# Loads issued when their buffers come free, and paired vector work, in a block-sparse attention and MoE kernel

## The chip, the cores and the metric

The kernel runs on one core of a Trainium2 chip. A time is the device time of one execution in microseconds (us); the time of a kernel is the median over its runs. Within a trace, times are counted from the first profiled instruction ("at 66.9" means 66.9 us after it), and the span is the time from there to the last one. The core has a matrix engine (TensorE, PE in the profile, with its weight loads as PEld), a vector engine (VectorE, DVE), an activation engine (ScalarE, ACT), a general one (GpSimd, POOL) and a queue that only issues transfers (SyncE, SP). Transfers run on 16 DMA engines.

## The reference

Four batches of 8 heads, 768 tokens, head size 64. Each token attends to the tokens less than 16 away and to 24 block rows: the maximum of the keys, and the mean of the values, over each block of 32 tokens. The result goes through a two-layer MLP with the quick GELU.

```python
B, H, S, D = q.shape                       # 4, 8, 768, 64
block, window = (32, 16)
k_sum = k.reshape(B, H, nb, block, D).max(axis=3)
v_sum = v.reshape(B, H, nb, block, D).mean(axis=3)
scores_l = scale * np.matmul(q, k.transpose(0, 1, 3, 2))
mask_l = np.abs(pos[:, None] - pos[None, :]) < window
scores_s = scale * np.einsum('bhsd,bhnd->bhsn', q, k_sum) + np.log(block)
a = softmax(concatenate([where(mask_l, scores_l, -1e9), scores_s]))
attn = np.matmul(a, concatenate([v, v_sum]))
h = x @ w_in                               # x = attn as (3072, 512); w_in 512 x 2048
out = (h * (1.0 / (1.0 + np.exp(-1.702 * h)))) @ w_out
```

All inputs are float32 in memory; all but the first keys are cast to bfloat16 or float16 as they are loaded.

## The kernel before

**Layout.** Heads go in four pairs p. For one batch, `kxs[s]` holds the transposed keys of all pairs as 12 tiles of 128 columns: 64 own columns, 32 halo columns copied from the neighbour tiles, and 24 block maxima in the rest (`s` is the batch modulo 2, so there are two such buffers, and likewise `qTs[s]` for queries and `vw[s]` for values). In `vw[s]` the halo rows and the block sums lie on the partitions beside the tile's own 64 tokens. One score product for a tile of 64 queries is then 64 columns, and one value product reads one such tile.

**Per batch,** the steps are: load k, q and v from memory with a cast; transpose keys and queries; fill the key halos and maxima (`rest_k`); fill the value halos by DMA (`halo_dmas`, four transfers), sum the value blocks on PE (`vsum`) and DVE (`block_sums`), and copy the sums into `vw[s]` by DMA (`sum_dmas`, two transfers); scores, exponential (ACT), mask (DVE), values (PE), norm (DVE), transposition of the result; first MLP layer (`ff_in`, `ff_one`), GELU (ACT), second layer (`ff_out`, `product`). `value_rows(s)` (line 1065) is the three steps on the values.

**Order.** Every engine's instructions run in the order in which they stand in the program (`_Ordered`, line 18), and each instruction waits only for what it reads or overwrites. So the attention of batch b+1 is written in between the MLP of batch b: in slots beside the second layer (`plan`, `beside`) and after blocks of the first layer (`todo` for batch 1, the loop from line 1112 for batches 2 and 3). In that loop `n // 2` counts eight blocks of the first layer, and `i` the 21 products of the second.

**Loads.** All k, q and v loads go out on POOL's queue: four transfers for k and q each, twelve for v (`load_turned`, `load_v`). POOL's queue is in order too, and no more than eight of its transfers are under way: each waits for the one eight before it. The buffers of k and q (`kb2`, `qb2`) are two tiles each, one per group g of two pairs, so a load of the next batch into group g waits until that group is transposed. `load_batch(b)` (line 242) issues k, v and q of a batch in a row. For batch 3 it holds them with small POOL copies that read a tile written later ("gates"): k waits for the query transpositions of batch 2 (`qTs[0]`), and q, issued in the loop (line 1133), for a result transposition (`xTT[1][1]`).

**Transpositions.** Batches 0 and 1 transpose on PE (`tk`, `tq`). Batches 2 and 3 use transposing DMAs on SP: `xk(g, s)` is two for the keys of a group, `xq(g, s)` one for its queries. SP also issues the halos, the block sums, the transpositions of results (`dx`) and the stores of the output, in order.

**Operand sums.** The second layer of batches 1 to 3, and most of the first of batch 3, work on sums of operands that save one product in eight: `g_sums(j)` (line 679) makes four sums of 128 x 384 for column block j on DVE, and `win_sum`, `w_sum` those of the weights.

Of the kernel before, what the change touches and what calls it, by code (L numbers as in the profile page):

```python
# [9 lines left out]
F32 = mybir.dt.float32  # L10
BF16 = mybir.dt.bfloat16
F16 = mybir.dt.float16
AX = mybir.AxisListType
# [22 lines left out]
def kernel(  # L36
# [82 lines left out]
    def load_turned(x, b, t2, name, gs_=(0, 1)):  # L119

        for g in gs_:
            t2[g] = castp2.tile([128, 2, NJ, 2, D], BF16, name=name, tag=name)
            for hh in range(2):
                h0 = hh * NP + 2 * g
                pool.dma_start(out=t2[g][:, :, :, hh].rearrange("p i a d -> p (i a) d"),
                               in_=x[b, h0:h0 + 2].rearrange("h (a p) d -> p (h a) d", p=128))

    def load_v(b):
        w5 = vw[b % 2].rearrange("p (j e) h c -> p j e h c", e=2)
        src = v[b].rearrange("h (j e p) d -> e j p h d", e=2, p=64)  # L130
# [108 lines left out]
        for g in range(4):  # L239
            eng.memset(v6[g * 32:g * 32 + nb, :, g, D:D + 1], float(block))  # L240

    def load_batch(b):
        if b == 3:
            pool.tensor_copy(out=gate2, in_=qTs[0][:, 0, 0:1])
        load_turned(k, b, kb2, "kb")
        if b == 3:
            pool.tensor_copy(out=gate2, in_=qTs[0][:, NP - 1, 0:1])
        if b == 1:
            load_turned(q, b, qb2, "qb", (0,))
        load_v(b)  # L250
        if b < 3:
            load_turned(q, b, qb2, "qb", (1,) if b == 1 else (0, 1))

    def load_w_in(n0, n1):
        wi = moe_w_in.rearrange("(ko ki) n -> ki ko n", ki=128)
# [82 lines left out]
    def at(ap, start, dims):  # L338
        a = ap[:, start:start + 1]
        return bass.AP(tensor=a.tensor, offset=a.offset, ap=[a.ap[0]] + dims)  # L340

    def flat_kx(p, s):
        return kx[p][s].rearrange("p t c -> p (t c)")

    def key_rows(p, s, ks, eng=dve, j0=0):
# [205 lines left out]
    def tk(p, s, eng):  # L551
        ps = psb.tile([128, 2048], BF16, name="ps_t", tag="big")[:, 0:S]
        turn_tiles(ps, kb2[p // 2][:, p % 2], NJ)
        copy(eng, at(flat_kx(p, s), 0, [[256, NJ], [192, 2], [1, 64]]),
             ps.rearrange("p (j e c) -> p j e c", e=2, c=64))
        rest_k(p, s, pool)

    def tq(p, s, eng):
        ps = pmm.tile([128, 1024], BF16, name="ps_t", tag="mm")[:, 0:S]
# [14 lines left out]
    def rest_k(p, s, eng=dve):  # L574
        ks = attp.tile([128, nb], BF16, name="ks", tag="ks")
        dve.tensor_reduce(out=ks.rearrange("p (j e n) -> p j e n", e=2, n=2),
                          in_=at(flat_kx(p, s), 0, [[256, NJ], [192, 2], [block, 2], [1, block]]),
                          axis=AX.X, op=ALU.max)
        key_halos(p, s, eng)
        key_rows(p, s, ks, eng)  # L580

    a_sb, x_sb, x2 = {}, {}, {}

# [13 lines left out]
    def values(b, half, g):  # L597

        if b == 1:
            banks = [pmm.tile([128, 512], F32, name="ps_av", tag="mm") for i in range(2)]  # L600
        else:
            ps = psb.tile([128, 1024], F32, name="ps_av", tag="big")
            banks = [ps[:, i * 512:i * 512 + 512] for i in range(2)]
        pvs = []
        for i in range(2):
            p = 2 * g + i
            a = a_sb[half, p]
            pv = banks[i][:, 0:390].rearrange("p (h j c) -> p h j c", h=2, j=JH)
            pvs.append(pv)
            for hh in range(2):  # L610
                for j in range(JH):
                    for e in range(2):
                        t = 2 * j + e
                        pe.matmul(out=pv[e * 64:e * 64 + 64, hh, j, :], lhsT=a[:, hh, t, :],
                                  rhs=vw[b % 2][:, half * TH + t, p + hh * NP if b else 2 * p + hh, 0:D + 1],
                                  start=True, stop=True, skip_group_check=True)
        x2[g] = attp.tile([128, 2, JH, 2, D], F16, name="x2", tag="x2", bufs=4)
        for i in range(2):
            norm(x2[g][:, :, :, i].rearrange("p h j d -> p j h d") if b else x2[g][:, i], pvs[i])

# [55 lines left out]
        gelu(half, nt, ph)  # L676


    def g_sums(j, eng=dve, which=(0, 1, 2, 3)):

        a1, a2 = gTb[:, j], gTb[:, j + NT // 2]
        l, r = slice(0, HALF), slice(HALF, S)
        for w in which:
            a, b_, op = {0: (a1[:, r], a2[:, r], ALU.add), 1: (gs[:, 0, j], a1[:, l], ALU.subtract),
                         2: (a1[:, l], a1[:, r], ALU.subtract), 3: (a2[:, l], gs[:, 1, j], ALU.subtract)}[w]
            eng.tensor_tensor(out=gs[:, w, j], in0=a, in1=b_, op=op)

    N1 = d_model // 2

# [180 lines left out]
            sp.dma_start(out=out[r0:r0 + 128, :], in_=osb)  # L870

    gate = consts.tile([128, 2], F32, name="gate")
    gate2 = consts.tile([128, 1], BF16, name="gate2")
    gate3 = consts.tile([128, 2], F32, name="gate3")
    dve.memset(gate, 0.0)

# [137 lines left out]
        key_rows(p, 0, ks0[:, p, 0:nb], dve, JH)  # L1014
    dve.memset(vw[1][:, :, :, D:VC], 1.0)
    clear_values(dve, 1)
    load_batch(1)


    plan0 = {1: ["q0", "q1", "q2"], 2: ["q3", "s0", "s1"], 4: ["s2", "s3"], 6: ["v0", "v1"], 8: ["x0"], 9: ["x1"]}  # L1020
# [63 lines left out]
    for i, (ms, part) in enumerate((ms, part) for part in range(4) for ms in range(JH)):  # L1084
        ff_out(0, ms, part)
        beside0(i)
        if i in (10, 11):
# [1 line left out]
            w_sum(i - 10, 1)  # L1089

    todo = {3: [lambda: tk(0, 1, act)], 4: [lambda: w_sum(2, 0)], 5: [lambda: tk(1, 1, act)],
            6: [lambda: w_sum(2, 1)], 7: [lambda: w_sum(3, 0)], 8: [lambda: tk(2, 1, act)], 
            10: [lambda: w_sum(3, 1)], 9: [lambda: tq(0, 1, dve)], 11: [lambda: tk(3, 1, act)], 12: [lambda: tq(1, 1, dve)],
            15: [lambda: value_rows(1)]}
    ff_in(1, range(3))
    for nt in range(3, NT):
        ff_in(1, (nt,))
# [4 lines left out]
    for i, (ms, part) in enumerate((ms, part) for ms in range(JH) for part in range(4)):  # L1102
        ff_out(1, ms, part)
        beside(1, i)
        if i == 2:
            load_batch(2)
        if i in (9, 11):
            xk(i // 2 - 4, 0)


    halves[0] = True
    for b in range(1, B - 1):
        nxt = b + 1 < B
        s = (b + 1) % 2
        if b == B - 2:
            for w in range(4):
                win_sum(w)
        for n in range(0, NT, 2):
            if n == 0:
                ff_open(order2[0:4], (lambda: tx(1, 1)) if b == 1 else None)  # L1120
            elif n == 2:
                for nt in order2[0:4]:
                    ff_one(1, nt)
                g_sums(0)
                g_sums(1)
            else:
                for nt in order2[n:n + 2]:
                    for half in range(2):
                        ff_one(half, nt)
                g_sums(n // 2, dve, (0, 1) if n + 2 == NT else (0, 1, 2, 3))  # L1130
            if nxt:
                if n == 0 and b > 1:
                    pool.tensor_copy(out=gate2, in_=xTT[1][1][:, 1, 0:1])
                    load_turned(q, b + 1, qb2, "qb")
                if n // 2 == 1:
                    value_rows(s)
                if n // 2 == 2 * b:
# [106 lines left out]
```

## Time and profile before

| | |
|---|---|
| median of 3 runs | 206.86 us (206.62 to 208.16) |
| the profiled execution | 206.51 us |
| its span, first to last instruction | 204.8 us |
| granted TensorE clock, mean | 0.998 |
| busy: PE, PEld, DVE, ACT, POOL | 198.1, 137.4, 140.4, 124.6, 92.7 us |
| moved by DMA | 27.93 MB, 95,851 packets, 83,649 of them under 512 bytes |

A busy figure is a sum of stretches in which an engine executes; matmuls overlap, and their ends are modelled. "Idle before" is the time in which an engine stood still before an instruction, with what ended it. The view of waits groups that by pairs of waiting and awaited work. The chain goes back from the last instruction to whatever released each step. The view of stretches gives the busy time of each engine in a piece of the span. A timeline row gives start, length, engine, operation, what is written and read, and a count. For a DMA the row shows its issue; the time to landing is from there to the last byte.

Stages by the trace: attention of the first token half of batch 0 until about 20 us; first layer on that half to 30; its second layer, with the attention of the other half beside it, to 45; first layer on the other half to 58, with the transpositions of batch 1; its second layer to 75, with the attention of batch 1; first layer of batch 1 to 97, with the keys and values of batch 2 made ready; products of batch 1 to 119, with the attention of batch 2; the same for batch 2 to 141 and 164; batch 3 to the end.

### The profile page before, as it was taken

What the parts mean: (1) busy time and instruction counts of PE and PEld (TensorE: products, weight loads), DVE (VectorE), ACT (ScalarE), POOL (GpSimd) and SP (SyncE); (2) the same over time, 40 slices, a digit from 0 to 9 for tenths busy, and PEclk for the clock granted to TensorE, in tenths of its full rate; (3) what the DMA queues carried; (4) which work ended last, traced back from release to release, by engine and by line L of the source; (5) the groups of instructions that cost most, each with busy time, mean ns of one, the idle gap of its engine ahead of it and who ended that gap; (6) DMA issues with size and microseconds to landing.
All of it is one profiled execution on the core that took longest, in us unless ns stands there. A gap on an engine that the chain in (4) does not pass through costs nothing.

```text
span 204.8 us, 5857 instructions
## 1 busy us (share of the span) xinstructions
PE 198.1 (97%) x2364; PEld 137.4 (67%) x2364; DVE 140.4 (69%) x388; ACT 124.6 (61%) x238; POOL 92.7 (45%) x144
## 2 busy tenths in 40 slices
PE   6989999999999999999999999999999999999992
PEld 6667654556754566665888975657888865578881
DVE  6767894594856874897768689896759546658211
ACT  4385876638786717777871546778661467983220
POOL 7965389555999584002965035000000019990000
PEclk9999999999999999999999999999999999999999
DMA  5999999999999999999999989996023730000222
GB/s 117 153 159 202 207 211 213 195 156 232 134 143 151 177 176 168 159 175 132 123 196 127 154 151 142 122 261 137 0 106 90 160 111 3 0 0 3 102 102 104
DMA packets 95851, 27.93 MB, mean 136 GB/s; under 512 B 83649, under 2 KB 92881, under 8 KB 95825
## 3 DMA queue, kind: packets, MB, share of 16 engines
q0 software_dynamic: 69920, 13.44, 85.2%
q1 hardware_dynamic: 25904, 14.13, 33.2%
q8 instruction: 18, 0.29, 0.6%
q14 instruction: 9, 0.07, 0.1%
HBM read 27.26 MB, written 6.29 MB: 164 GB/s over the span
## 4 chain that ended last, share of the span: by engine, by line
PE 90%; DMA 4%; POOL 2%; DVE 1%; issue 1%; ACT 0%; POOLq 0%; DVEq 0%
PE ph L28 33%; PE poA L28 16%; PE po L28 11%; PE poB L28 7%; PE ps_av L28 4%; DMA v0n<-in_v_dram 4%; PE poC L28 4%; PE phA L28 4%; PE ps_s L28 3%; PE ps_t L28 1%; PE ps_x L28 1%; POOL kb L28 1%; PE phB L28 1%; PE phC L28 1%; PE phE L28 1%; PE ps_vs L28 1%
## 5 line engine op out<-in xcount | busy, mean ns | idle before, releaser
L28 PE MATMUL ph<-xT,w_in_sb 128*128 128x384 f16 x416 | 70.2, 326 | 0.1
L28 PEld LDWEIGHTS <-w_in_sb 128*128 128x128 f16 x452 | 43.7, 98 | 27.8 <-issue 0.2
L28 ACT ACTIVATE gT<-ph 128x384 f16<-128x384 f32 x104 | 49.9, 492 | 18.5 <-PE ph L28 18.1
L28 PEld LDWEIGHTS <-gT 128*128 128x128 f16 x312 | 28.8, 98 | 11.3 <-issue 0.2
L28 ACT ACTIVATE a_sb<-ps_s 128x768 bf16<-128x768 f32 (+1 forms) x32 | 25.0, 826 | 12.5 <-PE ps_s L28 12.5
L28 POOL DMA_DIRECT2D vw<-in_v_dram x36 | 24.6, 700 | 12.4 <-DMA kb<-in_k_dram 4.8
L28 PEld LDWEIGHTS <-gs 128*128 128x128 f16 x288 | 27.7, 98 | 3.4
L28 POOL TENSOR_TENSOR gs<-gT 128x384 f16<-128x384 f16 x9 | 8.2, 911 | 42.3 <-ACT gT L28 42.3
L28 PE MATMUL po<-w_out_sb,gT 128*128 128x512 f16 x96 | 23.6, 380 | 0.0
L28 DVE TENSOR_TENSOR a_sb<-a_sb,mk 128x768 bf16<-128x768 bf16 x28 | 14.9, 554 | 6.5 <-ACT a_sb L28 5.9
L28 PE MATMUL poA<-ws,gs 128*128 128x256 f16 x144 | 18.7, 273 | 0.0
L28 DVE TENSOR_TENSOR x<-ps_av,rc 128x384 f16<-128x384 f32 x32 | 17.8, 558 | 1.1
L28 DVE TENSOR_TENSOR gs<-gT 128x384 f16<-128x384 f16 (+1 forms) x34 | 13.4, 394 | 7.2 <-ACT gT L28 6.9
L28 POOL DMA_DIRECT2D qb<-in_q_dram x16 | 15.1, 956 | 1.8 <-DMA w_in_sb<-in_moe_w_in_dram 1.1
L28 POOL DMA_DIRECT2D kb<-in_k_dram x15 | 14.5, 976 | 0.9 <-POOLq L1228 0.8
L28 PEld LDWEIGHTS <-kx 64*128 64x128 bf16 (+1 forms) x372 | 9.4, 95 | 6.8 <-issue 4.4
L28 DVE TENSOR_REDUCE ks<-kx 128x24 bf16<-128x768 bf16 x12 | 11.4, 949 | 3.4 <-ACT kx L28 3.2
L28 ACT ACT_TABLE_LOAD x10 | 12.8, 1283 | 1.0 <-PEq L1228 0.8
L28 ACT ACTIVATE osb<-poA 128x256 f32<-128x256 f32 x9 | 3.5, 384 | 16.0 <-PE poA L28 16.0
L28 ACT ACTIVATE s<-poA 128x256 f32<-128x256 f32 x11 | 4.2, 386 | 11.2 <-PE poA L28 11.2
L28 PEld LDWEIGHTS <-a_sb 128*64 128x64 bf16 (+2 forms) x400 | 7.8, 108 | 2.8 <-issue 1.3
L28 PE MATMUL poA<-ws,gT 128*128 128x256 f16 x72 | 9.3, 273 | 0.0
(117 smaller groups left out, 282.7 us busy)
## 6 DMA issues: line engine op xcount, KB each, us to landing
out_dram<-osb SPq DMA_DIRECT2D x23, 256.0 KB, 3.3
kb<-in_k_dram POOLq DMA_DIRECT2D x15, 192.0 KB, 7.1
qb<-in_q_dram POOLq DMA_DIRECT2D x12, 192.0 KB, 10.9
vw<-in_v_dram POOLq DMA_DIRECT2D x36, 64.0 KB, 5.7
w_out_sb<-in_moe_w_out_dram POOLq DMA_DIRECT2D x4, 512.0 KB, 13.0
w_in_sb<-in_moe_w_in_dram POOLq DMA_DIRECT2D x3, 512.0 KB, 12.9
vw<-vs SPq DMA_DIRECT2D x6, 198.0 KB, 6.1
v0n<-in_v_dram POOLq DMA_DIRECT2D x4, 192.0 KB, 8.1
```

The lines of the kernel that those rows point to most:

```text
L28: r = f(*a, **kw)
```

## The change

- `load_batch` and both gates are gone. `load_k(b, g...)`, `load_q(b, g...)` and `load_v(b)` are called where the buffers come free. Batch 1's loads keep place and order. Batch 2: v before the first layer of token half 1 of batch 0, k after the transpositions of batch 1's keys (group 0 at block 7, group 1 at block 12 of that layer), q in the place where `load_batch(2)` was. Batch 3: k and q in the first layer of batch 1 (`n // 2` = 0 and 2), v where `load_batch(3)` was.
- On SP, `xk` for batches 2 and 3 stands after products 4 and 7 of the second layer (it was 9 and 11, and 16 and 18), and both `xq` at the start of the next first layer, ahead of `value_rows` (they were at `n // 2` = 2 and 4, behind it).
- `rest_k` (one pair) becomes `rest_k2` (two pairs at once): one maximum over 128 x 1536 and three halo copies on DVE, then one `key_rows` per pair on DVE. For batch 1, halos and rows were on POOL, and the four calls stood in `tk`; now two calls stand at blocks 7 and 13.
- `g_sums` can make two column blocks at once: blocks 0 and 1, 2 and 3, 4 and 5 are paired. `values` for batches 2 and 3 norms two pairs with one reciprocal and one product.

```diff
-    def load_batch(b):
-        if b == 3:
-            pool.tensor_copy(out=gate2, in_=qTs[0][:, 0, 0:1])
-        load_turned(k, b, kb2, "kb")
-        if b == 3:
-            pool.tensor_copy(out=gate2, in_=qTs[0][:, NP - 1, 0:1])
...
+    def load_k(b, *gs_):
+        load_turned(k, b, kb2, "kb", gs_)
+
+    def load_q(b, *gs_):
+        load_turned(q, b, qb2, "qb", gs_)
...
+    def rest_k2(g, s):
+        flat = kxs[s].rearrange("p i t c -> p (i t c)")
+        o, n = 2 * g * NQ * 128, 2 * NJ
+        ks = attp.tile([128, 2, nb], BF16, name="ks", tag="ks")
+        dve.tensor_reduce(out=ks.rearrange("p i (j e n) -> p (i j) e n", e=2, n=2),
+                          in_=at(flat, o, [[256, n], [192, 2], [block, 2], [1, block]]),
+                          axis=AX.X, op=ALU.max)
+        dve.tensor_copy(out=at(flat, o + 256 + 96, [[256 * NJ, 2], [256, NJ - 1], [1, 16]]),
+                        in_=at(flat, o + 256 - 16, [[256 * NJ, 2], [256, NJ - 1], [1, 16]]))
...
+        for i in range(2):
+            key_rows(2 * g + i, s, ks[:, i])
...
              ps.rearrange("p (j e c) -> p j e c", e=2, c=64))
-        rest_k(p, s, pool)
...
+        if b > 1:
+            pv = ps.rearrange("p (i c) -> p i c", i=2)[:, :, 0:390].rearrange("p i (n c) -> p i n c", c=D + 1)
+            rc = attp.tile([128, 2, 2 * JH, 1], F32, name="rc2", tag="rc2")
+            dve.reciprocal(out=rc, in_=pv[..., D:D + 1])
+            dve.tensor_mul(x2[g].rearrange("p h j i d -> p i (h j) d"), pv[..., 0:D],
+                           rc.to_broadcast([128, 2, 2 * JH, D]))
+            return
...
-    load_batch(1)
+    load_k(1, 0, 1)
+    load_q(1, 0)
+    load_v(1)
+    load_q(1, 1)
...
-            6: [lambda: w_sum(2, 1)], 7: [lambda: w_sum(3, 0)], 8: [lambda: tk(2, 1, act)], 
-            10: [lambda: w_sum(3, 1)], 9: [lambda: tq(0, 1, dve)], 11: [lambda: tk(3, 1, act)], 12: [lambda: tq(1, 1, dve)],
+            6: [lambda: w_sum(2, 1)], 8: [lambda: tk(2, 1, act)], 
+            7: [lambda: w_sum(3, 0), lambda: rest_k2(0, 1), lambda: load_k(2, 0)],
+            10: [lambda: w_sum(3, 1)], 9: [lambda: tq(0, 1, dve)], 11: [lambda: tk(3, 1, act)],
+            12: [lambda: tq(1, 1, dve), lambda: load_k(2, 1)], 13: [lambda: rest_k2(1, 1)],
             15: [lambda: value_rows(1)]}
+    load_v(2)
     ff_in(1, range(3))
...
         if i == 2:
-            load_batch(2)
-        if i in (9, 11):
-            xk(i // 2 - 4, 0)
+            load_q(2, 0, 1)
+        if i in (4, 7):
+            xk(i // 3 - 1, 0)
...
-                g_sums(0)
-                g_sums(1)
+                g_sums(0, n=2)
...
-                g_sums(n // 2, dve, (0, 1) if n + 2 == NT else (0, 1, 2, 3))
+                if n // 2 in (3, 5):
+                    g_sums(n // 2 - 1, n=2)
+                elif n // 2 > 5:
+                    g_sums(n // 2, dve, (0, 1) if n + 2 == NT else (0, 1, 2, 3))
             if nxt:
-                if n == 0 and b > 1:
-                    pool.tensor_copy(out=gate2, in_=xTT[1][1][:, 1, 0:1])
-                    load_turned(q, b + 1, qb2, "qb")
+                if n == 0:
+                    xq(0, s)
+                    xq(1, s)
+                    if b == 1:
+                        load_k(3, 0, 1)
                 if n // 2 == 1:
                     value_rows(s)
-                if n // 2 == 2 * b:
-                    xq(0, s)
-                    xq(1, s)
-                if n // 2 in (2, 3, 4, 5):
-                    rest_k(n // 2 - 2, s)
+                if n // 2 == 2 and b == 1:
+                    load_q(3, 0, 1)
+                if n // 2 in (2, 4):
+                    rest_k2(n // 4 - 1, s)
...
             if nxt and b + 2 < B:
                 if i == 1:
-                    load_batch(b + 2)
-                if i in (16, 18):
-                    xk(i // 2 - 8, b % 2)
+                    load_v(b + 2)
+                if i in (4, 7):
+                    xk(i // 3 - 1, b % 2)
```

More of the change, by code (lines that the diff above doesn't have):

```diff
@@ L240, in clear_sums @@
             eng.memset(v6[g * 32:g * 32 + nb, :, g, D:D + 1], float(block))
-    def load_batch(b):
-        if b == 3:
-            pool.tensor_copy(out=gate2, in_=qTs[0][:, 0, 0:1])
-        load_turned(k, b, kb2, "kb")
-        if b == 3:
-            pool.tensor_copy(out=gate2, in_=qTs[0][:, NP - 1, 0:1])
[L248 to L252, printed above, removed]
+    def load_k(b, *gs_):
+        load_turned(k, b, kb2, "kb", gs_)
+    def load_q(b, *gs_):
+        load_turned(q, b, qb2, "qb", gs_)
     def load_w_in(n0, n1):
@@ L343, in flat_kx @@
         return kx[p][s].rearrange("p t c -> p (t c)")
+    def rest_k2(g, s):
[7 more added lines that the diff above has]
+                        in_=at(flat, o + 256 - 16, [[256 * NJ, 2], [256, NJ - 1], [1, 16]]))
+        dve.tensor_copy(out=at(flat, o + 128 + 48, [[256 * NJ, 2], [256, NJ - 1], [1, 16]]),
+                        in_=at(flat, o + 256, [[256 * NJ, 2], [256, NJ - 1], [1, 16]]))
+        dve.tensor_copy(out=at(flat, o + 128 + 32, [[256, n], [-48, 2], [1, 16]]),
+                        in_=at(flat, o + 48, [[256, n], [144, 2], [1, 16]]))
+        for i in range(2):
+            key_rows(2 * g + i, s, ks[:, i])
     def key_rows(p, s, ks, eng=dve, j0=0):
@@ L572, in xq @@
                      in_=qb2[g].rearrange("p i a h d -> p (i a h d)"), transpose=True)
[L574 to L580, printed above, removed]
     a_sb, x_sb, x2 = {}, {}, {}
@@ L676, in ff_one, with g_sums @@
         gelu(half, nt, ph)
-    def g_sums(j, eng=dve, which=(0, 1, 2, 3)):
-        a1, a2 = gTb[:, j], gTb[:, j + NT // 2]
+    def g_sums(j, eng=dve, which=(0, 1, 2, 3), n=1):
+        j1, j2 = slice(j, j + n), slice(j + NT // 2, j + NT // 2 + n)
+        a1, a2 = gTb[:, j1], gTb[:, j2]
         l, r = slice(0, HALF), slice(HALF, S)
         for w in which:
-            a, b_, op = {0: (a1[:, r], a2[:, r], ALU.add), 1: (gs[:, 0, j], a1[:, l], ALU.subtract),
-                         2: (a1[:, l], a1[:, r], ALU.subtract), 3: (a2[:, l], gs[:, 1, j], ALU.subtract)}[w]
-            eng.tensor_tensor(out=gs[:, w, j], in0=a, in1=b_, op=op)
+            a, b_, op = {0: (a1[:, :, r], a2[:, :, r], ALU.add), 1: (gs[:, 0, j1], a1[:, :, l], ALU.subtract),
+                         2: (a1[:, :, l], a1[:, :, r], ALU.subtract),
+                         3: (a2[:, :, l], gs[:, 1, j1], ALU.subtract)}[w]
+            eng.tensor_tensor(out=gs[:, w, j1], in0=a, in1=b_, op=op)
     N1 = d_model // 2
@@ L872 @@
     gate = consts.tile([128, 2], F32, name="gate")
-    gate2 = consts.tile([128, 1], BF16, name="gate2")
     gate3 = consts.tile([128, 2], F32, name="gate3")
```

## The prediction

> **What bounds the kernel now.** The first view is the page's row of busy times.
>
> ```profile
> PE 198.1 (97%) x2364; PEld 137.4 (67%) x2364; DVE 140.4 (69%) x388; ACT 124.6 (61%) x238; POOL 92.7 (45%) x144
> ```
>
> PE is busy nearly throughout, but busy matmuls can still be waiting ones, so the next two views ask whether PE ever waits: its own waits, in full, and the stretches.
>
> ```profile
> PE ps_h L28 <- DVE warm L28: 1.3, 1, 1.3
> PE ps_vt L28 <- DMA v0n<-in_v_dram: 0.6, 1, 0.6
> PE ps_s L28 <- DVE qT L28: 0.4, 1, 0.4
> PE ps_k L28 <- ACT kb L28: 0.3, 1, 0.3
> ```
>
> ```profile
> 76.00:97.00 21.00, 21.00 (x184) 12.65 (x183) 15.86 (x54) 14.89 (x31) 4.17 (x6) 1.00 1.65 159
> ...
> sum 180.00, PE 179.56 PEld 123.47 DVE 126.05 ACT 113.61 POOL 77.22; mean PE 19.95 PEld 13.72 DVE 14.01 ACT 12.62 POOL 8.58
> ```
>
> PE waits four times in the whole run, each time for something of batch 0: the warm-up tile, the first keys, the first values, and its late queries. The sum covers 20 to 200 us: 0.44 us of 180 are idle. The clock of the stretch is 1.00. Last, the chain in order of time, for the pace and for the dates by which something must be ready.
>
> ```profile
> 34.18 0.57 DVE qT L28
> ...
> 80.74 0.53 PE ps_vs L28 x48
> 81.27 15.71 PE ph L28 x96
> 96.98 0.46 PE ps_s L28 x24
> ...
> 108.83 0.88 PE ps_av L28 x48
> ```
>
> The late queries' wait is at 34, ahead of the first changed instruction. 96 matmuls of 384 columns in 15.71 us are 164 ns each, that is 2.3 columns a nanosecond with nothing between them. This stretch is where DVE is fullest and where the DMAs of batch 2 run, and neither slows it. So **PE's own instructions are the time**; a wait that goes on another engine is worth nothing unless PE stood behind it.
>
> The Trainium skill, page "Perfetto Trace Analysis", section "Identifying the Most-Contended Engine", says that matmul busy time doesn't tell how near PE is to its limit and that weight-load busy time (here PEld) should be used. By it 67% would leave a third of PE's time open to better feeding. The trace disagrees at 164 ns a matmul; what the rule would make of the time is the third rival.
>
> **The change part by part.** It removes, adds or reorders no PE instruction from the first to the last: the transposes, scores, sums and products stand in the same slots. So the gain is bounded by the idle 0.44 us between 20 and 200, none of it behind a changed instruction: I take 0 (bounds 0 and -0.4). What is left to price is whether something arrives later than PE asks for it.
>
> *Operand sums, norms, later halos.* The groups of DVE between 84.5 and 96.9, and one group of the whole run.
>
> ```profile
> L28 DVE TENSOR_REDUCE ks<-kx 128x24 bf16<-128x768 bf16 x4 | 3.8, 948 | 0.0
> L28 DVE TENSOR_TENSOR gs<-gT 128x384 f16<-128x384 f16 x10 | 3.5, 354 | 0.6 <-ACT gT L28 0.5
> L28 DVE COPY kx<-kx 128x80 bf16<-128x80 bf16 x8 | 1.0, 172 | 0.0
> L28 DVE COPY kx<-ks 128x288 bf16<-128x288 bf16 x4 | 0.9, 230 | 0.0
> L28 DVE COPY kx<-kx 128x192 bf16<-128x192 bf16 x4 | 0.8, 196 | 0.0
> ```
>
> ```profile
> L28 DVE TENSOR_TENSOR a_sb<-a_sb,mk 128x768 bf16<-128x768 bf16 x28 | 14.9, 554 | 6.5 <-ACT a_sb L28 5.9
> ```
>
> A two-input operation of 768 columns takes 554 ns (the masks), two of 384 take 708. Merging four pairs saves 0.6 us, and with three merges in each of two batches 3.7 us of DVE. The norm merge is alike and smaller. All of it is hidden under PE: priced at 0. The pairing delays the sums of blocks 2 and 4 by one block, but the products that read them come after block 7, so nothing waits.
>
> *Batch 1's key maxima and halos leave POOL for DVE.* The rows of POOL, DVE, SP and PE in order of time show what they held up and what follows.
>
> ```profile
> 53.45 2.04 POOL L28 DMA_DIRECT2D qb<-in_q_dram  x2
> 55.53 0.75 POOL L28 COPY kx<-kx 128x80 bf16<-128x80 bf16 x3
> ...
> 59.76 4.05 POOL L28 DMA_DIRECT2D kb<-in_k_dram  x4
> ```
>
> ```profile
> 56.51 0.55 DVE L28 COPY qT<-ps_t 128x768 bf16<-128x768 bf16 x1
> 58.23 0.29 DVE L28 COPY vpart<-ps_vs 128x128 f32<-128x128 f32 x1 [1.18 <-PE ps_vs L28]
> 58.56 1.18 DVE L28 TENSOR_TENSOR vs<-ps_vs,vpart 32x128 bf16<-32x128 f32 x4
> ```
>
> ```profile
> 55.53 2.69 SPq L28 DMA_DIRECT2D vw<-vw  x4
> 59.77 1.24 SPq L28 DMA_DIRECT2D vw<-vs  x2
> ```
>
> ```profile
> 55.20 0.50 PE L28 MATMUL ps_t<-wide,qb 128*128 128x128 bf16 x6
> ...
> 60.30 0.50 PE L28 MATMUL ps_t<-wide,qb 128*128 128x128 bf16 x6
> ...
> 66.93 0.57 PE L28 MATMUL ps_av<-vw,a_sb 128*64 128x65 bf16 x24
> ```
>
> DVE's second query copy is held by PE's transposes, which end at 55.7, so it runs 55.75 to 56.3 (today at 56.51, behind a single maximum). The second paired maximum follows it. No row has that shape; its cost lies between one of today's, 0.95, and two, 1.90, and I take 1.8, near two, because the copies above show time growing with columns. The three copies cost 0.5 to 1.1 (once or twice 2 x 0.172 + 0.196), I take 0.6; two key rows 0.46. That is 2.9 us: DVE is free at 59.2, and the block sums (0.29 + 1.18) end at 60.7 instead of 59.74. The first of the two copies of sums into the value buffer leaves at 60.7, the second at 61.35 (half of 1.24 later).
>
> *Twelve value loads of batch 2 move ahead of its keys.* POOL is free at 55.5 instead of 59.76 and starts them there, twelve at 0.7 us each (24.6 for 36 in the row below), to 63.9, then the keys' four (4.05, to 68) and the queries' four (to 72). No instruction of PE needs them before 80.7. What they meet are the transfers that PE does need: batch 1's four value halos (issued 55.5 to 58.2) and the two sums, which must have landed when the values start at 66.93. The rows for the loads and, one query each, for three pairs of sums:
>
> ```profile
> L28 POOL DMA_DIRECT2D vw<-in_v_dram x36 | 24.6, 700 | 12.4 <-DMA kb<-in_k_dram 4.8
> ```
>
> ```profile
> DMA to landing us min/median/max: 3.0/4.3/5.6
> DMA to landing us min/median/max: 5.3/5.5/5.7
> DMA to landing us min/median/max: 9.0/9.3/9.7
> ```
>
> The first query is these two sums today: the first met almost no load (3.0), the second the first key load (5.6), and it landed at 66.0, 0.9 us ahead of PE. The second is batch 0's sums, half as large, under a full stream of loads; the third is batch 2's, behind four halos and two transposing DMAs. After the change the second sum leaves at 61.35, and with 5.6 to 6.2 it lands between 66.95 and 67.55. PE then waits 0 to 0.6 us; **I take 0.3**. The ends are 0 (at 5.5 it is just in time) and 4.1 (at 9.7, 71.05); I stay near 5.5 because no transposing DMA is ahead of these two.
>
> A rule bears on that end. The Trainium skill's page "DMA: Bandwidth & Descriptors", section "Queues, rings and completion order", says that each DMA engine takes turns between the queues at packet granularity. By it loads on POOL's queue could at most double the 3.0 of an undisturbed sum, giving 6.0, a landing at 67.35 and a wait of 0.4; the 9.7 would then need work ahead in SP's own queue.
>
> A smaller neighbour is the last query load of batch 1, by the page's rows of landings and the query on these two loads:
>
> ```profile
> kb<-in_k_dram POOLq DMA_DIRECT2D x15, 192.0 KB, 7.1
> ...
> DMA to landing us min/median/max: 4.6/5.1/5.6
> ```
>
> The second query load leaves at 54.5 (half of 2.04 after 53.45) and lands 5.6 later, at 60.1; PE's next transposes start at 60.30. The new loads stand behind it in POOL's queue, so I price that at 0, with 0.3 as the bad end.
>
> *SP's order for batch 2.* The key transposes now stand ahead of two output stores and wait for keys of which the second leaves at 64.9 and lands 7.1 later, at 72; today that is 60.8 + 7.1 = 68. The stores behind them wait too, but there are three output buffers, and the fourth output is written only by the products after 97. Both query transposes stand ahead of the halos. SP's rows today, and the landing of batch 2's queries:
>
> ```profile
> 79.83 2.69 SPq L28 DMA_DIRECT2D vw<-vw  x4
> 84.03 1.24 SPq L28 DMA_DIRECT2D vw<-vs  x2
> 88.39 7.45 SPq L28 DMA_TRANSPOSE qT<-qb  x2
> ```
>
> ```profile
> DMA to landing us min/median/max: 8.6/13.8/16.3
> ```
>
> The queries, issued until 72, land with today's 16.3 at worst at 88; two transposes of up to 3.7 us each, halos 2.7 and sums 1.2 bring SP to 99.3 in the bad case, 94 in the likely one; with 9.3 the sums land at 103 to 109 against 108.83. Priced at 0, bad end 0.2. The second query transpose, which today leaves SP by 95.84 for scores from 96.98 on, is then earlier. On POOL the keys of batch 3 now wait for batch 2's key transposes to have read their buffers, and its queries for the query transposes; behind both stand only the values of batch 3, wanted in the first layer of batch 2. These loads fill 80 to 100 beside the halos and sums above, which is why I keep 9.3 for those.
>
> **Sum.** 206.51 (profiled: 204.8 span and 1.7 around it) + 0.3 = 206.8. The median of the runs shown is 0.35 above the profiled one; so 207.2.
>
> **Rivals.**
> First, **the value rows of batch 1 come late**, which ends slower. Place: PE at 66.93. Price: landing minus 66.93, up to 4.1 us, 211.0; it costs 1% (2.07 us) once the second sum needs over 7.7 us, and about 209 is its middle. For it: 9.0 to 9.7 at batch 2. Against: nothing transposes yet at 61. Chance 0.18, two thirds of it above 1%.
> Second, **the loads start no earlier**, because buffers or the eight-transfer limit hold them. The limit waits on queries that land at 60.1, so two or three value loads could be held to about 60; the sums then meet what they meet today, and only DVE's 0.95 us is left, against a margin of 0.9: 206.9. Chance 0.12.
> Third, **PE is paced by its feeding** (by the Trainium skill's rule above), with DVE as the engine that paces it in the first layers of batches 1 and 2. The saved 3.7 us would then come off: 203.2. Against it stand 164 ns and the empty list of waits. Chance 0.03.
>
> **Chances.** The forecast, a wait of 0 to 1 us, has 0.67. The first rival covers 1 to 4. The range 206.4 to 209.1 takes in the idle 0.4 below the median and the first rival to its middle. Within 1% is 204.8 to 208.9, about what this measurement can tell from no change: 0.85; faster 0.03, from the third rival; slower 0.12, from the first.
>
> **What would show it.** Right: PE's waits list gains at most a short one, value products on a DMA into `vw` at 67; POOL's first value load of batch 2 starts at 55.5; the block sums of batch 1 end near 60.7; the stretch 76 to 97 still has 21.00 of PE. Wrong: PE waiting over 2 us at 67 or at 109, or 96 matmuls in clearly less than 15.7 us.

## The result, and the profile after

The changed kernel takes 214.02 us (median of 4 runs, 213.33 to 218.22) against 206.79 (4 runs, 206.62 to 208.16) on the same chip: a ratio of 1.033, with a 95% interval of 1.027 to 1.038. It is slower, and above the predicted range. Ratios here leave disturbed executions out, so one can be smaller than the medians beside it suggest. The profiled execution took 214.60 us with a span of 212.9, so 8.1 us of span are to be found.

The page's row of busy times, after:

```profile
PE 200.2 (94%) x2364; PEld 137.9 (65%) x2364; DVE 136.4 (64%) x340; ACT 124.5 (58%) x238; POOL 87.1 (41%) x125
```

PE executes the same 2364 instructions. DVE has 48 fewer and 4.0 us less, POOL 5.6 us less. So the vector work that was to go is gone; the time isn't. The view of stretches shows where PE stood still. Its columns are the stretch, its length, the busy time of PE, PEld, DVE, ACT and POOL, then the granted clock, the DMA share and GB/s. First after:

```profile
58.00:66.00 8.00, 6.49 (x127) 3.60 (x116) 4.97 (x16) 4.86 (x8) 6.11 (x10) 1.00 2.09 164
...
76.00:97.00 21.00, 21.00 (x193) 12.79 (x186) 15.76 (x36) 13.78 (x29) 6.18 (x7) 1.00 1.98 165
...
119.00:132.00 13.00, 8.92 (x53) 5.39 (x51) 5.81 (x7) 3.92 (x8) 2.71 (x4) 0.87 1.64 185
...
124.50:128.00 3.50, 3.50 (x17) 1.88 (x15) 3.46 (x5) 0.38 (x1) 0.02 (x1) 0.54 1.89 164
```

and the one stretch that matters most, before:

```profile
119.00:132.00 13.00, 13.00 (x127) 7.96 (x126) 12.05 (x30) 8.48 (x19) 4.83 (x5) 1.00 1.88 125
```

Two places: 58 to 66, and above all 119 to 132, where PE is idle for 4.1 us in all and in between runs 3.5 us at a clock of 0.54. PE's waits name what it stood behind (the list's other rows are of batch 0, as before):

```profile
PE poA L28 <- DVE osb L28: 3.1, 1, 3.1
PE ps_t L28 <- DMA qb<-in_q_dram: 1.5, 1, 1.5
...
PE ph L28 <- DMA xT<-x: 0.9, 1, 0.9
```

The rows of PE in order of time give the sum (start, length, instruction, count, idle before it):

```profile
62.28 0.49 PE L28 MATMUL ps_t<-wide,qb 128*128 128x128 bf16 x6 [1.51 <-DMA qb<-in_q_dram]
...
68.90 0.91 PE L28 MATMUL ps_av<-vw,a_sb 128*64 128x65 bf16 x24
...
119.21 1.04 PE L28 MATMUL poA<-ws,gs 128*128 128x256 f16 x8
120.08 1.04 PE L28 MATMUL poB<-w_out_sb,gs 128*128 128x256 f16 x8
124.25 1.38 PE L28 MATMUL poA<-ws,gT 128*128 128x256 f16 x8 [3.13 <-DVE osb L28]
125.42 4.64 PE L28 MATMUL ph<-xT,w_in_sb 128*128 128x384 f16 x18
131.00 2.44 PE L28 MATMUL ph<-xT,w_in_sb 128*128 128x384 f16 x14 [0.94 <-DMA xT<-x]
```

The query transposes of batch 1 start at 62.28 instead of 60.30: **2.0**. The first value products at 68.90 take 0.91 instead of 0.57: **0.3**. The eight products at 119.21 take 0.87 to the next start; the eight at 120.08 need as much, so the next could have started at 120.95 and start at 124.25: **3.3**. The eight from 124.25, at the halved clock in part, take 1.17 to the next start: **0.3**. The 18 matmuls from 125.42 would take 2.95 at 164 ns each, and the next starts 5.58 later: **2.6**, about half of it the halved clock and half the wait for `xT`. That is 8.5, against 8.1 of span. Of the 2.0, 0.3 was there before anything changed: the transpositions that stood at 55.20 stand at 55.50.

This sum is PE's time; it does not say what each part would save alone. The chain of this stretch, in order of time, goes from PE's products at 119 through SP's queue to the last result transposition:

```profile
121.39 9.57 DMA xT<-x
...
131.00 2.44 PE ph L28 x14
```

Without the wait for the output tile, PE would have come to the products at 131.00 at about 124.8 at the earliest (120.95, 0.87 for eight products and 2.95 for 18, an estimate from the rows above), and would have waited there for `xT` until 131.00. So in this execution the late transposition alone is enough for the loss from 121 to 131; the output tile and the half clock lie beside it.

What PE waited for at 121 was DVE, and DVE waited itself. Its row on the output tile:

```profile
123.77 0.42 DVE L28 TENSOR_TENSOR osb<-poA,s 128x256 f32<-128x256 f32 x1 [3.74 <-DMA out_dram<-osb]
```

An output sum may not be written before the store that last read its buffer has landed, and there are three such buffers. So PE stood behind DVE, DVE behind a store, and the store behind other transfers. The view of transfers from 95 to 121 shows it (an issue's operation, count, KB, and median us to landing; the DMA row is the busy share in tenths, in 40 slices). After:

```profile
DMA  9999999999999999999199999999999399999999
...
out_dram<-osb SPq DMA_DIRECT2D x4, 256.0 KB, 8.9
...
kx<-kb SPq DMA_TRANSPOSE x4, 10.1
xT<-x SPq DMA_TRANSPOSE x3, 9.7
```

Before:

```profile
DMA  2999199999999999999999999999299906997876
...
out_dram<-osb SPq DMA_DIRECT2D x4, 256.0 KB, 3.9
...
xT<-x SPq DMA_TRANSPOSE x4, 2.8
```

Output stores take 8.9 us instead of 3.9, the transpositions of results 9.7 instead of 2.8. The DMA engines have almost no pause. The rows of SP and POOL show what is new among them, SP first:

```profile
95.48 6.67 SPq L28 DMA_TRANSPOSE kx<-kb  x2
...
106.66 3.31 SPq L28 DMA_TRANSPOSE kx<-kb  x2
110.06 0.60 SPq L28 DMA_DIRECT2D out_dram<-osb  x1
```

```profile
93.47 2.04 POOL L28 DMA_DIRECT2D qb<-in_q_dram  x2 [3.72 <-DMA qT<-qb]
98.22 2.01 POOL L28 DMA_DIRECT2D qb<-in_q_dram  x2 [2.70 <-DMA qT<-qb]
...
123.84 0.68 POOL L28 DMA_DIRECT2D vw<-in_v_dram  x1 [2.01 <-DMA vw<-in_v_dram]
```

The same two queues before, SP first:

```profile
119.37 6.29 SPq L28 DMA_TRANSPOSE kx<-kb  x4
```

```profile
107.10 3.40 POOL L28 DMA_DIRECT2D vw<-in_v_dram  x5 [0.40 <-PE poB L28]
...
121.69 4.07 POOL L28 DMA_DIRECT2D qb<-in_q_dram  x4
```

Batch 3's queries are now loaded from 93 to 100, not from 121.7 on; its values are issued until 124.5 instead of 110.5; and its four key transpositions, which went out from 119.4, now begin at 95 and stand among the stores of batch 1. All of this is batch 3's part of the change. What SP issued from 95 to 122 landed in the order of its issue in this execution: the second pair of key transpositions at 116.4 and 117.6, then the store issued at 110.06 at 119.5, and so on to the last transposition of results at 131.0.

### The profile page after: what moved, and what is told of

It is laid out like the page before. It is cut to its first block, busy times and chain, and to the rows that moved or that the text cites. A ratio compares the mean times of both kernels' runs of the same rounds, so it can differ in the third digit from the quotient of the medians.

```text
span 212.9 us, 5785 instructions
## 1 busy us (share of the span) xinstructions
PE 200.2 (94%) x2364; PEld 137.9 (65%) x2364; DVE 136.4 (64%) x340; ACT 124.5 (58%) x238; POOL 87.1 (41%) x125
## 4 chain that ended last, share of the span: by engine, by line
PE 79%; DMA 12%; DVE 3%; POOL 2%; issue 1%; SPq 1%; ACT 0%; POOLq 0%; DVEq 0%
PE ph L28 30%; PE poA L28 15%; PE po L28 7%; PE poB L28 7%; DMA xT<-x 4%; PE ps_av L28 4%; DMA v0n<-in_v_dram 4%; DMA vw<-vs 4%; PE poC L28 4%; PE phA L28 4%; PE ps_s L28 2%; PE ps_x L28 1%; POOL kb L28 1%; PE ps_t L28 1%; PE phB L28 1%; PE phC L28 1%
## 5 line engine op out<-in xcount | busy, mean ns | idle before, releaser
L28 PE MATMUL ph<-xT,w_in_sb 128*128 128x384 f16 x416 | 71.9, 330 | 1.0 <-DMA xT<-x 0.9
L28 DVE TENSOR_TENSOR gs<-gT 128x768 f16<-128x768 f16 (+2 forms) x22 | 11.5, 524 | 13.6 <-ACT gT L28 13.6
L28 DVE TENSOR_TENSOR x<-ps_av,rc 128x384 f16<-128x384 f32 (+1 forms) x24 | 16.6, 690 | 0.8
L28 DVE TENSOR_REDUCE ks<-kx 128x48 bf16<-128x1536 bf16 x6 | 10.5, 1748 | 2.5 <-ACT kx L28 2.4
```

The costliest lines, as they stand in the source:

```text
L28: r = f(*a, **kw)
```

## The experiments

Times are medians, each beside that of the kernel before on the same chip. The diffs are against the changed kernel unless something else is said.

**First group: which part.** Three theories stood. L: the released loads keep the DMA engines busy, so stores and result transpositions land late. T: the order on SP's queue does it. D: the paired vector work makes the output sums late.

*e1: batch 3's loads and transpositions as before.*

```diff
-                if n == 0:
+                if n == 0 and b == 1:
                     xq(0, s)
                     xq(1, s)
-                    if b == 1:
-                        load_k(3, 0, 1)
...
-                if i in (4, 7):
-                    xk(i // 3 - 1, b % 2)
+                if i in (16, 18):
+                    xk(i // 2 - 8, b % 2)
```

with both gates of `load_batch(3)` and batch 3's `xq` back in their places.

> The change without its part for batch 3: keys and queries of batch 3 behind the gates again, their transposing DMAs at the old places. Theory L (the released loads keep the DMA engines busy until 133, so output stores and result transpositions land late): the waits at 121 to 131 go (3.3 + 1.3 at half clock + 1.3), the two at 60 to 69 (1.7 + 0.35) stay: about 208.5. Theory T (the order on SP's queue alone): the same here. Theory D (the paired vector work makes the output sums late): about 214, no change.

207.84 us against 207.82; ratio 1.001 (0.997 to 1.004). The whole loss is in batch 3's part. D falls: the pairs are all here, and DVE's busy time is 4.8 us less than in the kernel before, without any gain in time. The page's row of busy times, and the one wait of PE behind batch 0 that the kernel before had not:

```profile
PE 198.0 (96%) x2364; PEld 137.6 (67%) x2364; DVE 135.6 (66%) x340; ACT 124.5 (61%) x238; POOL 88.3 (43%) x128
```

```profile
PE ps_av L28 <- DMA vw<-vs: 1.0, 1, 1.0
```

*e2: batch 2's loads as before (k, v, q in a row), batch 3 as changed.*

```diff
-    load_v(2)
...
         if i == 2:
+            load_k(2, 0, 1)
+            load_v(2)
             load_q(2, 0, 1)
```

(and without the `load_k(2, ...)` in `todo`).

> The change with the loads of batch 2 in their old place and order (keys, values, queries, after the third block of the second layer). L: the wait of 1.7 at 60 and of 0.35 at 69 go, batch 3's waits stay or grow, because the same transfers start 4 us later: 211.5 to 214. T and D: the waits at 60 to 69 go as well, the rest stays as it is: 212.

216.67 against 207.82; ratio 1.034 (1.022 to 1.046). Not faster than the changed kernel, and in the profile PE waits 3.0 us for an output tile and another 3.0 for the block sums `vw<-vs`. The new load order of batch 2 is not what costs.

*e3: the merges alone.* Every load and transposition has its old place; only `rest_k2`, the paired `g_sums` and the paired norm are left of the change.

> All loads and transposing DMAs at their old places, only the paired sums, norms, halos and key maxima stay. L and T: the time of before, 206.4 to 207.2, since PE waits for nothing that the pairs make. D: 209 or more.

212.12 against 207.82; ratio 1.020 (1.013 to 1.027): slower, with every transfer in its old place in the program. PE's waits, then the stretch behind them, then POOL's row:

```profile
PE ps_av L28 <- DMA vw<-vs: 3.3, 2, 1.7
```

```profile
71.40:76.00 4.60, 4.57 (x77) 2.72 (x78) 2.49 (x7) 2.57 (x4) 4.60 (x7) 0.50 1.72 112
```

```profile
56.11 4.06 POOL L28 DMA_DIRECT2D kb<-in_k_dram  x4
```

Batch 2's key loads start at 56.11 instead of 59.76. In the kernel before, POOL's halo and row copies of batch 1 stood ahead of them for 4.2 us. With those copies gone the loads run into the block sums of batch 1, which PE is waiting for. e7 below puts this to the test.

*e4: three output stores of batch 1 left out* (the first, second and third of its six; those rows of the output stay unwritten).

```diff
+            if b == 1 and (t, o) in ((0, "o1"), (0, "o2"), (1, "o1")):
+                now.pop((t, o))
+                return
             sp.dma_start(
```

> The change, with three output stores of batch 1 left out (both of token tile 0, the first of tile 1), so that no output buffer waits for a store to land. Its output lacks those rows. L and T: the wait of PE for the output sums at 121 (3.1) and the half clock behind it (1.3) go, but the result transpositions land when the DMA engines get to them, so part of it comes back as a longer wait for them: 209.5 to 212. D (the vector engine itself is late): no change, about 214.

The runs spread from 208.14 to 215.91 (median 214.42 against 207.82); ratio 1.009 (1.003 to 1.014). In the profiled execution, 210.11 us, the waits for an output tile and for `xT` and the half clock are gone; so a buffer held by a store was that wait. The stretch, and a new wait ahead of it, for nothing that the profile shows:

```profile
119.00:132.00 13.00, 13.00 (x139) 9.14 (x138) 8.47 (x14) 7.69 (x16) 0.24 (x1) 1.00 1.43 194
```

```profile
118.29 0.92 PE L28 MATMUL poB<-ws,gs 128*128 128x256 f16 x7 [1.47 <-issue]
```

Six of the ten runs took over 214 us, as long as the changed kernel, and the ratio rests on the others; what held these six no profile shows. So e4 shows what held DVE in one execution, not what the stores cost.

**Second group: loads or order.**

*e5: the kernel before, with batch 3's key and query loads released alone.*

```diff
-        if b == 3:
-            pool.tensor_copy(out=gate2, in_=qTs[0][:, 0, 0:1])
-        load_turned(k, b, kb2, "kb")
+        if b < 3:
+            load_turned(k, b, kb2, "kb")
...
-                if n == 0 and b > 1:
-                    pool.tensor_copy(out=gate2, in_=xTT[1][1][:, 1, 0:1])
-                    load_turned(q, b + 1, qb2, "qb")
+                if n == 0 and b == 1:
+                    load_turned(k, 3, kb2, "kb")
...
                     xq(1, s)
+                    if b == 1:
+                        load_turned(q, 3, qb2, "qb")
```

> The kernel before with one edit: the key loads of batch 3 issue at the start of the first layer of batch 1 and its query loads after the query transposes of batch 2, without gates; every result transpose, the query and key transposes and the vector work keep their old places. Theory L (the released loads keep the DMA engines busy, so output stores and result transposes land late): the waits of about 3 us for an output tile and 1 us for xT in 117 to 131 come back, with the half clock behind them; 211 to 215 us. Theory T (what counts is the order on SP's queue, key and query transposes ahead of result transposes and stores): SP's order is the old one, 206.5 to 208.5 us.

210.32 against 207.69; ratio 1.017 (1.011 to 1.024). Slower, but not where L said: no output tile and no `xT` is late. PE waits at 99.9 and 104.6 for the query transpositions of batch 2:

```profile
PE ps_s L28 <- DMA qT<-qb: 2.3, 2, 1.8
```

From 84 to 105 these two take 11.3 us to land, before 5.6; the views of transfers, e5 and then before:

```profile
qT<-qb SPq DMA_TRANSPOSE x2, 11.3
```

```profile
qT<-qb SPq DMA_TRANSPOSE x2, 5.6
```

The released loads do make short transfers late, those that are due at that time. (In the changed kernel these two transpositions take 9.7 us to land, but leave SP from 84.1 on, not from 88.4, and PE did not wait for them.)

*e6: the changed kernel with batch 3's `xk` and `xq` at their old places; its loads stay released.* *e10: only `xk` back.* *e11: one of the two `xk` back.*

```diff
-                if i in (4, 7):
-                    xk(i // 3 - 1, b % 2)
+                if i in (16, 18):
+                    xk(i // 2 - 8, b % 2)
```

That is e10; e11 has `if i in (4, 18): xk(i // 18, b % 2)`, and e6 also moves `xq` of batch 3 back to `n // 2 == 4`.

> The changed kernel with the key transposes of batch 3 back behind products 16 and 18 and its query transposes back in the middle of the first layer of batch 2; its loads stay released. Theory L: 211 to 215 us, an output tile still late by some 3 us at 117 to 125. Theory T: 206.5 to 208.5 us. If both have a share, 208.5 to 211.

> The changed kernel with only the key transposes of batch 3 back behind products 16 and 18; the query transposes stay at the start of batch 2's first layer. If the four key transposes between 95 and 110 are what makes the changed kernel slow: 206.5 to 208.5 us, as with both moved back. If the query transposes have a part: above 209.

> The changed kernel with the first two key transposes of batch 3 early and the other two behind product 18. If the delay grows with each transpose ahead of the stores: a wait for an output tile or xT of some 1 to 2 us in 117 to 131, 208.5 to 211.5 us. If there is slack for two of them: no wait, 206.5 to 208.5.

e6: 207.12 against 207.69, ratio 1.000 (0.996 to 1.003). e10: 208.28 against 207.72, ratio 1.001 (0.998 to 1.004). e11: 209.47 against 207.72, ratio 1.006 (1.003 to 1.010), with 1.4 us of waiting for `xT`. L alone falls with e6 and e10: the loads are released, and no output tile and no `xT` is late. One pair of key transpositions ahead of the stores already makes PE wait, so there is no slack for it, though the times of e10 and e11 alone, whose intervals overlap, would not show it. The views of transfers of e10 and e11, 95 to 121:

```profile
xT<-x SPq DMA_TRANSPOSE x4, 4.3
```

```profile
xT<-x SPq DMA_TRANSPOSE x4, 7.1
```

*e8: batch 3's key and query loads left out* (its transpositions read what batch 2 left, so batch 3's output is of other data). *e12: only the query loads left out* (the same for its queries).

```diff
-                    if b == 1:
-                        load_k(3, 0, 1)
...
-                if n // 2 == 2 and b == 1:
-                    load_q(3, 0, 1)
```

(e8; e12 takes the last two lines alone.)

> The changed kernel without the key and query loads of batch 3 (its transposes read what batch 2 left in the buffers; everything else runs). Theory L: 2 MB less to move between 85 and 133, the DMA engines have idle time before 125, the waits for an output tile and for xT at 117 to 131 vanish; 206 to 209 us. Theory T: the transposes still stand ahead of the stores on SP; 211 to 215 us.

> The changed kernel without the query loads of batch 3 (its query transposes read what batch 2 left); key loads, value loads and all transposes stay early. If released bytes and early transposes add up in the same DMA engines, 0.75 MB less of the loads that were added (half of them) brings the output wait at 121 from 3.3 us to 0 to 1 and the time to 207 to 210 us. If the early key transposes alone did it, 211 to 215.

e8: 207.94 against 207.69, ratio 1.002 (1.000 to 1.005). e12: 208.06 against 207.43, ratio 1.001 (0.998 to 1.004). T alone falls too: all transpositions are early in both, and no output tile and no `xT` is late. The views of transfers of e8 and e12:

```profile
DMA  9999999999999995099989910009679902999802
...
out_dram<-osb SPq DMA_DIRECT2D x6, 256.0 KB, 3.1
...
xT<-x SPq DMA_TRANSPOSE x4, 3.0
```

```profile
xT<-x SPq DMA_TRANSPOSE x4, 5.5
```

So it takes both, released bytes and early transpositions, and together they cost more than the sum of the two: over the 2.8 us of before, a result transposition lands 0.2 later with the early transpositions alone (e8), 1.5 with the released loads alone (e10), and 6.9 with both. The counterpart of e12, the key loads left out, was not run. Put in order of how long a result transposition took to land, before is at 2.8, e8 3.0, e10 4.3, e12 5.5, e11 7.1 and the changed kernel 9.7. Of these, PE waits for it at 7.1 and 9.7; in e13 below it does not at 9.2, where it comes late itself.

*e9: the stores of batch 1 on ACT's queue.*

```diff
-            sp.dma_start(out=out[r0:r0 + 128, cols], in_=now[t, o][:, cols])
+            (act if b == 1 else sp).dma_start(out=out[r0:r0 + 128, cols], in_=now[t, o][:, cols])
```

> The changed kernel with the six output stores of batch 1 issued by ScalarE instead of SyncE; loads and transposes as changed. Theory Q (in one queue what is issued first lands first, so the stores and result transposes wait for the four key transposes ahead of them on SP): the stores pass them, no output tile is late at 121, the half clock behind it goes, at most the 1 us for xT is left; 207 to 210 us. Theory B (the DMA engines are full between 97 and 121, whoever issues): the stores still land 8 to 10 us after issue and the 3 us wait stays; 212 to 215.

The runs are 211.31 to 219.52 (4 runs, against 207.72); ratio 1.023 (1.014 to 1.032), so neither theory has the time clearly. In the profiled one, 211.31 us, the wait for an output tile is gone and 0.8 us for `xT` is left. This execution lost about 3.1 us before any of that, in batch 0: from 10 to 30 PE's clock was 0.82 and 0.84, and the first value products of batch 1 stand at 70.06, not at 66.93. From there to the block sums of batch 3 it takes 60.0 us (to 130.10), the kernel before 57.8 (66.93 to 124.74) and the changed kernel 64.5 (68.90 to 133.37). So 4.4 of the 6.7 us went with the queue, in one execution. But the stores, in a queue of their own, still take long:

```profile
out_dram<-osb ACTq DMA_DIRECT2D x4, 256.0 KB, 7.1
...
xT<-x SPq DMA_TRANSPOSE x4, 7.9
```

Of the 5.0 us by which a store was late (8.9 against 3.9), 1.8 went with the queue in this execution and 3.2 stayed. How much of the loss is SP's order and how much the shared engines is therefore only partly separated. The Trainium skill, page "DMA: Bandwidth & Descriptors", section "Queues, rings and completion order", says that SP's and ACT's queues are rings on the same 16 engines; the 7.1 agrees.

**The merges again, and the changed kernel again.**

*e7: e3 with a gate.* Against e3:

```diff
         if i == 2:
+            pool.tensor_copy(out=gate2, in_=kxs[1][:, NP - 1, 0, 64:65])
             load_k(2, 0, 1)
```

> The merges alone, as in the run e3, with one POOL copy of 128x1 ahead of batch 2's key loads that reads the key rows of batch 1's last pair. If the copies of halos and rows that the merges took off POOL had held these loads back until 59.8, the waits for vw<-vs at 67 to 71 (3.3 us in e3) fall to 0 to 0.6 and the time is 206.0 to 208.0 us. If the merged vector work itself costs e3 its 4 us, it stays at 211 to 213.

207.72 against 207.69; ratio 1.001 (0.997 to 1.005). POOL's rows:

```profile
59.10 0.19 POOL L28 COPY gate<-kx 128x1 bf16<-128x1 bf16 x1 [3.44 <-DVE kx L28]
59.62 4.06 POOL L28 DMA_DIRECT2D kb<-in_k_dram  x4 [0.33 <-issue]
```

One copy of 0.19 us that only waits takes back all of e3's loss. What POOL's copies had done for the kernel before was to hold the loads until 59.8.

*e13: the changed kernel once more.*

> The changed kernel once more, on this chip. If the wait for the query load of batch 1 at 60 belongs to the change, it is there again with 1 to 1.7 us; if it was the disturbance of one execution, it is 0 to 0.5 us (0 to 0.4 in six other kernels with the same instructions up to there). The waits for an output tile at 121 and for xT at 129 are there in either case, 2 to 5 us together; 211 to 216 us.

214.10 (4 runs, 210.15 to 215.77) against 207.43. The wait for an output tile is there with 2.9 us. The expected one for `xT` is not: with the half clock the 32 products from 125.73 take 6.7 us instead of 5.2, and 1.0 us of waiting for batch 3's values follows at 134. The wait for batch 1's query load at 60 is not there either. e12's profiled execution, with the same instructions up to there, had it with 1.8 us, so it belongs to some executions only. It goes with the date of the loads: they were issued at 54.77 in the changed kernel's first profile and at 55.51 in e12, but at 53.95 here.

No version was faster than the kernel before by more than can be measured, as the 0.4 us of idle PE in the prediction would have it.

## Why the prediction was wrong

- **What bounds the kernel: right.** PE waits nowhere else, 76 to 97 still has 21.00 busy, and DVE's 4.8 us less in e1 gained nothing. The third rival, that PE is paced by its feeding, falls with that.
- **Operand sums, norms, halos: hidden, right.** The guess for the paired maximum, 1.8 us, measured 1.75. The block sums of batch 1 end at 60.44 (59.26 and four in 1.18), predicted 60.7:

```profile
56.51 1.74 DVE L28 TENSOR_REDUCE ks<-kx 128x48 bf16<-128x1536 bf16 x1
...
59.26 1.18 DVE L28 TENSOR_TENSOR vs<-ps_vs,vpart 32x128 bf16<-32x128 f32 x4
```

- **The maxima's move off POOL: a half of it not seen.** The step priced DVE's delay. That POOL's copies also dated the loads behind them was in the quoted rows (55.53 to 59.76, then `kb`), and the second part of the step used that date for the values; but the loads' earlier start was never named as the cost of the merge itself. e3 gives it, 4.3 us (212.12 against 207.82), and e7 takes it back.
- **Value loads of batch 2 ahead, second sum late by 0.3: the right place, the wrong size.** The second sum was to land 5.6 to 6.2 us after its issue; the two took 7.9 in the median, and PE lost 0.3 only because it was itself 2.0 late; that this agrees with the forecast 0.3 is luck. Where it was not late, in e1, the wait was 1.0 us (the value products start at 66.86 and go on at 68.09, 1.2 behind 66.93), inside the first rival's 1 to 4; e13 has 1.3, e10 1.5, e6 and e8 0.4. By the rule that an engine takes turns between queues, quoted in the prediction, 6.0 was the most unless work stood ahead in SP's own queue. 7.9 exceeds it, and no transposition stood ahead, but the four halos did: they left from 56.68, and the later ones took 6.6 to 7.2 us to land. So this does not decide on the rule:

```profile
vw<-vs SPq DMA_DIRECT2D x2, 198.0 KB, 7.9
```

- **The smaller neighbour, priced at 0 with 0.3 as the bad end: 1.5 us in this execution.** The loads behind it in POOL's queue were taken to leave it alone, and most of the delay is not theirs: the query loads left at 54.77 instead of 53.45, behind value loads of batch 1 that the change leaves as they were, and the second took 6.4 us to land instead of 5.6. It is a cost of some executions only (e12, not e13); why the loads leave later in these stays open.
- **The second rival, that the loads start no earlier: true in part.** Seven of the twelve value loads left from 56.78 to 61.6, the other five were held until 62.66 to 66.86, and the keys left from 68.00, not 63.9. The seven met the block sums all the same.
- **SP's order: the step that failed.** It was worked out for batch 2 alone, and that came true. For batch 3 it ended with "behind both stand only the values of batch 3, wanted in the first layer of batch 2. These loads fill 80 to 100". Two things are wrong there. First, each transfer was judged by its own deadline in its own queue; what the released loads did to the stores and result transpositions of 97 to 131 has no term in the sum, and the loads went on to 124, not 100. Second, batch 3's key transpositions, which the change moves ahead of batch 1's stores, are not in the step at all. The remark on three output buffers, made for the stores of batch 2's stage, was the right question: at 119 and 121 the fifth and the sixth output of batch 1 did wait for stores. The term, 0 in the sum, measured 6.2 us (3.3, 0.3 and 2.6), all of it within the time in which the last result transposition was under way.
- **A term that no step had:** the half clock behind a long wait, about 0.3 and 1.3 us of PE's time, here in the shadow of that transposition.
- **"What would show it"** named, as signs of being wrong, waits of over 2 us at 67 and 109. The long one came at 121. Of the signs of being right, 21.00 and 60.7 came true, while the value loads began at 56.78, not 55.5.

The runs settle the cause as a combination: with the transpositions late (e6, e10) or half of the released loads gone (e12) the 7 us vanish, and with all loads out too (e8); the loads released alone in the old order cost 1.7% (e5), with PE's new waits elsewhere.

## What to carry to other kernels

A gate on a load is not only a date before which it may not run: it keeps the DMA engines free for the short transfers that the busy engine waits for soon. When a load is released or a transposition moved, take the landing times of everything issued in the stretch into which it moves, stores that hold a buffer included, from the nearest stretch of the trace in which the DMA row shows no pause. And an instruction that is taken off a queue was also a delay for what stands behind it there; if that is a load, put the date back with a small copy that waits.

## What was not expected of the hardware

- The same 256 KB store lands after 3.1 us with pauses in the DMA row (e8) and after 8.9 with almost none (after); a result transposition after 2.8 to 9.7.
- In the changed kernel PE's clock was halved for 3.5 us (0.54) behind an idle time of 3.1 us, and in e3 behind two waits of 1.7 and 1.6 us with one product between them (0.50 over 4.6 us); there it fell at 70.3, 2.4 us after PE's last full work at 67.9. Single waits of 1.5 us (the changed kernel at 60) and 1.8 us (e5, e12) left it at 1.00. The Trainium skill, page "TensorE: Matmul & The Clock Gate", in its part 1 on the clock gate, puts the limit at an idle window of about 3.4 us. The measured stretches are shorter, so here less than that was enough.
- PE stood 1.5 us for nothing that the profile shows, in e4 at 118, amid full DMA engines.
